# A gated-MLP kernel whose order a planner writes: transposes of the identity in TensorE's planned waits, another clock model in the planner, other due times

## Chip, cores and metric

The kernel runs on one core of one Trainium2 chip. The metric is the device time of one execution in microseconds (us), lower is better; the time before is the median of three runs.

## What is computed

The inputs are float32. Attention over q, k, v of shape (4, 8, 576, 64): heads 0 to 3 see the last 32 positions, heads 4 to 7 every fourth of the last 128. Its output, as 2304 rows of 512, goes through two gated MLPs with inner width 1536:

```python
attn = softmax(where(mask, q @ k.T / 8, -1e9)); x = attn @ v          # rows: (batch, position)
x = x / sqrt(mean(x * x) + 1e-6) * rms_g
x = (silu(x @ w_gate) * (x @ w_val)) @ w_out                          # first MLP
out = (sigmoid(x @ w2_gate) * (x @ w2_val)) @ w2_out                  # second MLP
```

The weights come as 64-bit numbers and are converted to float32 on the chip.

## The kernel before

**The planner.** Nothing is issued in the order in which it is written. Each piece of work is added with `add(engine, cost, fn, reads, writes, tiles, due)` to a `Line`. `emit()` then walks a planned time: for each engine it takes the piece that can start first by the planned costs, among equals the one with the lowest `due`, calls its function, and so fixes the order of that engine's instructions. On the chip the engines run these orders with semaphores; a piece whose data are late holds up all that stands behind it on its engine. A tile comes from a ring of a few buffers and can be taken when its last reader is done. `clocked` lengthens a planned piece of TensorE while the planner believes the engine's clock to be low. All due times and costs that can be set are in `PARAMS`; due times count in planned microseconds from the first MLP step, so that negative ones lie before it.

**The stages.** (1) Attention in 48 groups (batch, pair of heads, third of the sequence). A group is twelve small products for the scores (`scores`, L780), mask and maximum on VectorE (L791), exp on ScalarE (L797), a reciprocal (L804, L805), a scaling (L810), three transposes on TensorE (`turn`, L824) with a copy out (L828), twelve products with v (`values`, L836), and a copy to `xT` (L847, L855). The keys and queries of the first batch are turned by TensorE (`first_qk`, L618 the loads, L631 the transposes, L642 the copies out), those of the other batches by VectorE (`attn_load`, L739, L753). v is loaded at L692 (the dilated heads) and L702, L710 (the others). (2) `x_norm` normalises 384 rows: squares (L880), sums (L896), a reciprocal root on VectorE or GpSimd, spread and turned (L952), then scaled and split in two parts (L964, L488, L492). (3) The first MLP in 6 chunks of 384 rows times 12 steps (`mlp_step`: gate and value products, L1055; `y_group`: output products, L1092). It starts when ten groups are done, and the other groups are woven between its products. (4) The second MLP with a fast product scheme (`unit`, L1240, L1256), then the output.

**Weights.** `words` loads a weight of 512 KB into one of three buffers `wst` (L446, L450), and ScalarE (L466), VectorE (L472 to L481) and then ScalarE and GpSimd (L488, L492) convert and split it. The first twelve have the due times `wload + wload_step * n` for their loads.

**Queues.** Nearly all loads are issued by SyncE (SP), in one order. Those of the first batch have the due times `ld_b` (head pair 3), `ld_a` (head pair 2), `ld_v` (v of the dilated heads), `ld_c` (head pair 0, v 10 later) and `ld_d` (head pair 1, v 6 later).

**Warm-up.** `warm_up` puts 18 products of zeros ahead of all, and offers 19 more lots of five at set times, each of which is dropped if TensorE is busy then.

Of the kernel before, what the change touches and what calls it, by code (L numbers as in the profile page):

```python
# [24 lines left out]
PARAMS = {  # L25
    "margin": 1091.18, "wait": 0.691, "w_sq": 0.926, "w_hi": 1.192, "w_lo": 1.258, "x_hi": 0.315,
    "x_lo": 0.378, "h_hi": 0.2, "h_lo": 0.034, "qk": 0.603, "norm": 0.665, "pts": 12.624,
    "o": 0.023, "snap": 41.721, "h_ahead": 45.667, "h2_ahead": 61.961, "evac": 97.928,
    "holds": (6, 6), "norm_act": 0.209, "slack": 0.0, "share_v": 0.6, "share_p": 0.33, "cold": 1.7,
# [5 lines left out]
    "ld_a": -469.296, "ld_b": -609.198, "ld_v": -251.427, "ld_c": -222.082, "ld_d": -395.339,  # L35
    "lead": -8.213, "xdue": 0.69, "wdue": -6.094, "wslope": 2.935, "wload": -554.115,
    "wload_step": 36.279, "warm_n": 18, "warm_t": 13.382, "warm_dt": 0.858, "warm_c": 19,
    "warm_m": 5, "warm_late": 0.481, "warm_due": 42.437, "mask_cost": 0.18, "exp_cost": 0.36,
    "s_cost": 0.65, "o_cost": 0.56, "t_cost": 0.33,
# [29 lines left out]
class Op:  # L69
    __slots__ = ("eng", "cost", "fn", "tiles", "due", "lat", "preds", "succs", "left", "end",  # L70
                 "seq", "release", "ways", "until", "bus", "ahead", "start", "dense")


class Line:
# [8 lines left out]
    TAIL = {"PE": 0.16, "DVE": 0.085, "ACT": 0.085, "PL": 0.035}  # L83
    AFTER = {"PE": -0.16, "DVE": 0.034, "ACT": 0.034, "PL": 0.078}

    def __init__(self):
        self.ops, self.writer, self.readers = [], {}, {}
        self.now = self.bus = 0.0
        self.last, self.mate, self.longer = {}, {}, 0.0
        self.work, self.window, self.warm = 0.0, 0, True  # L90
# [21 lines left out]
    def clocked(self, start, cost, dense):  # L112

        span = 3.413
# [149 lines left out]
def attention_then_two_gated_mlps(  # L264
# [15 lines left out]
    nc = tc.nc  # L280
# [1217 lines left out]
```

## Time and profile before

| what | value |
| --- | --- |
| runs | 1043.42, 1040.94, 1042.42 us |
| median | 1042.42 us |
| the profiled execution | 1040.54 us, of which its span 1038.8 us |
| TensorE busy | 996.5 us, 96% of the span |
| mean granted clock of TensorE | 0.977 |

The span is the time from the first to the last instruction on the chip; 1.7 us lie around it. A granted clock of 1.00 is TensorE's 2.4 GHz, 0.50 its 1.2 GHz. An engine that counts as busy at the lower clock needs about twice the time for the same work.

### The profile page before, as it was taken

To read this page: it belongs to the slowest core of one execution; us is meant where nothing else is said; L and a number is where in the kernel's file an instruction comes from. 1 tells how busy PE (TensorE), PEld (TensorE's weight loads), DVE (VectorE), ACT (ScalarE), POOL (GpSimd) and SP (SyncE) were. 2 spreads that over 40 slices of the span, in tenths; PEclk is the share of its full clock that TensorE was granted. 3 is DMA by queue.
4 is the path that set the end of the run, shared out by engine and by line. 5 is a ranking of instruction groups with operands and counts; after the bars stand their busy time and mean duration, and the time that the engine had idled before them with its cause. 6 is when DMAs were issued, how large, how long until landed. Compare 5 with 4: busy or idle time off the path is not lost.

```text
span 1038.8 us, 19924 instructions
## 1 busy us (share of the span) xinstructions
PE 996.5 (96%) x7222; PEld 961.8 (93%) x7222; DVE 680.4 (66%) x1461; ACT 468.9 (45%) x1273; POOL 492.6 (47%) x631
## 2 busy tenths in 40 slices
PE   4889989999999999999999989999999999999997
PEld 4768788888999999999999989999999999999996
DVE  5588865476884487767776487558656587466633
ACT  4786755565432443222222455446443354434331
POOL 4365764443732662112213685548545388334410
PEclk9669999999999999999999999999999999999999
DMA  8848646484577476686672332213241334134234
GB/s 184 179 100 202 141 111 161 80 251 111 196 230 263 150 270 220 227 287 230 202 253 84 100 107 75 74 64 112 65 146 60 134 113 155 54 108 122 59 80 92
DMA packets 192978, 152.04 MB, mean 146 GB/s; under 512 B 135760, under 2 KB 164432, under 8 KB 192880
## 3 DMA queue, kind: packets, MB, share of 16 engines
q1 hardware_dynamic: 192880, 150.77, 49.9%
q8 instruction: 57, 0.93, 0.4%
q14 instruction: 41, 0.34, 0.1%
HBM read 103.55 MB, written 47.19 MB: 145 GB/s over the span
## 4 chain that ended last, share of the span: by engine, by line
PE 79%; DVE 6%; SPq 4%; DMA 3%; POOL 3%; issue 2%; ACT 2%; DVEq 0%; POOLq 0%; ACTq 0%
PE y L1092 24%; PE g L1055 13%; PE v L1055 13%; PE att L1240 9%; PE g L1240 7%; PE v L1240 6%; PE att L780 2%; SPq L692 1%; PE att L836 1%; PE att L824 1%; DMA wst<-in_moe_w_val_dram 1%; SPq L618 1%; DVE S L567 1%; DVE t L1272 1%; SPq L739 1%
## 5 line engine op out<-in xcount | busy, mean ns | idle before, releaser
L1092 PE MATMUL y<-h,wo 128*128 128x288 f32 (+1 forms) x2016 | 369.6, 313 | 1.4 <-DVE h L495 1.2
L1092 PEld LDWEIGHTS y<-h,wo 128*128 128x128 f32 x2016 | 318.3, 188 | 3.7 <-DVE h L495 1.5
L492 POOL TENSOR_TENSOR h<-t,h 128x288 fp32r<-128x288 f32 (+1 forms) x131 | 129.1, 987 | 305.0 <-ACT h L488 293.7
L1055 PE MATMUL g<-xo,w 128*128 128x384 f32 x864 | 166.1, 340 | 0.0
L1055 PE MATMUL v<-xo,w 128*128 128x384 f32 x864 | 163.0, 336 | 0.0
L1055 PEld LDWEIGHTS g<-xo,w 128*128 128x128 f32 x864 | 151.7, 190 | 1.9 <-issue 0.4
L1055 PEld LDWEIGHTS v<-xo,w 128*128 128x128 f32 x864 | 150.2, 188 | 0.6
L488 ACT CAST h<-t 128x288 fp32r<-128x288 f32 (+1 forms) x152 | 70.6, 468 | 152.3 <-DVE t L1073 85.3
L1240 PE MATMUL att<-xo,w 128*128 128x288 f32 x576 | 92.1, 295 | 0.0
L1067 ACT ACTIVATE t<-g 128x384 f32<-128x384 f32 x72 | 35.3, 490 | 114.6 <-PE g L1055 114.6
L1240 PEld LDWEIGHTS att<-xo,w 128*128 128x128 f32 x576 | 81.5, 188 | 0.0
L1256 DVE TENSOR_TENSOR t<-t,att 128x288 f32<-128x288 f32 x96 | 43.0, 448 | 51.5 <-PE att L1240 49.6
L1069 DVE SCALAR_TENSOR_TENSOR t<-t,g 128x384 f32<-128x384 f32 x72 | 39.7, 551 | 53.3 <-ACT t L1067 52.8
L810 POOL TENSOR_SCALAR pr<-pr,rs 128x96 f32<-128x96 f32 x115 | 47.2, 427 | 49.5 <-DVE rs L805 37.5
L1240 PE MATMUL v<-xo,w 128*128 128x288 f32 x396 | 63.6, 296 | 3.0 <-DVE t L1256 2.1
L472 DVE TENSOR_SCALAR wz<-wz 128x512 f32<-128x512 f32 x72 | 39.7, 551 | 40.3 <-ACT wz L466 40.2
L492 POOL TENSOR_TENSOR xo<-xq,xo 128x576 fp32r<-128x576 f32 x33 | 50.7, 1544 | 30.6 <-ACT xo L488 18.6
L1240 PE MATMUL g<-xo,w 128*128 128x288 f32 x396 | 63.4, 295 | 0.5 <-DVE t L1256 0.5
L466 ACT ACTIVATE wz<-wst 128x512 f32<-128x512 f32 x71 | 47.4, 668 | 36.3 <-DMA wst<-in_moe_w_gate_dram 14.2
L797 ACT ACTIVATE pr<-pr,nmx 128x96 f32<-128x96 f32 x144 | 52.4, 366 | 19.0 <-DVE nmx L791 19.0
L478 DVE SCALAR_TENSOR_TENSOR wz<-wst,wz 128x512 int32<-128x512 int32 x72 | 59.2, 824 | 1.3
L1240 PEld LDWEIGHTS v<-xo,w 128*128 128x128 f32 x396 | 55.8, 188 | 3.9 <-DVE t L1256 2.8
(164 smaller groups left out, 1625.2 us busy)
## 6 DMA issues: line engine op xcount, KB each, us to landing
z<-wz SPq DMA_DIRECT2D x54, 256.0 KB, 2.5
wst<-in_moe_w_gate_dram SPq DMA_DIRECT2D x24, 512.0 KB, 4.6
wst<-in_moe_w_val_dram SPq DMA_DIRECT2D x24, 512.0 KB, 4.7
wst<-in_moe_w_out_dram SPq DMA_DIRECT2D x24, 512.0 KB, 4.2
xq<-y SPq DMA_DIRECT2D x20, 576.0 KB, 4.6
x<-xo SPq DMA_DIRECT2D x12, 768.0 KB, 4.3
xo<-x SPq DMA_DIRECT2D x12, 768.0 KB, 5.9
z<-z SPq DMA_DIRECT2D x36, 256.0 KB, 2.7
```

Of the source, the lines that this page charges most:

```text
L466: add("ACT", act(CW), lambda: nc.scalar.activation(out=z.t.bitcast(F32), in_=top().bitcast(F32), func=ACTF.Square), reads=[("wst", key)], ...
L472: add("DVE", Shared(0.33), lambda: nc.vector.tensor_scalar(out=z.t.bitcast(F32), in0=z.t.bitcast(F32), scalar1=LEAST * LEAST, scalar2=MANT ...
L478: add("DVE", Shared(0.595), lambda: nc.vector.scalar_tensor_tensor(out=z.t, in0=top(), scalar=-0x40000000, in1=z.t, op0=ALU.bitwise_and, o ...
L488: add("ACT", act(n), lambda: nc.scalar.copy(out=hi(), in_=src()), reads=reads, writes=[key] + [order] * bool(order), tiles=tiles + [dst], ...
L492: add("PL", pool(n), lambda: nc.gpsimd.tensor_tensor(out=lo(), in0=src(), in1=hi().bitcast(F32), op=ALU.subtract), reads=reads, writes=[ke ...
L797: add("ACT", PARAMS["exp_cost"], lambda u=u: nc.scalar.activation(out=pr.t[:, u], in_=pr.t[:, u], func=ACTF.Exp, bias=nmx.t[:, u:u + 1], s ...
L810: add("PL", Shared(0.305), lambda u=u: nc.gpsimd.tensor_scalar(out=pr.t[:, u], in0=pr.t[:, u], scalar1=rs.t[:, u:u + 1], scalar2=1.0, op0= ...
L1055: nc.tensor.matmul(out=bank.t, lhsT=w[:, l, cols], rhs=x[:, r, j], start=kk == 0 and n == 0, stop=kk == KD - 1 and n == 2)
L1069: add("DVE", dve(T1), lambda: nc.vector.scalar_tensor_tensor(out=t.t, in0=t.t, scalar=1.0, in1=gb.t, op0=ALU.add, op1=ALU.mult), writes=[k ...
L1092: nc.tensor.matmul(out=yb.t, lhsT=w.t[:, l, s], rhs=h.t[:, r], start=n == 0 and j == 0, stop=n == nf - 1 and j == 2)
L1240: nc.tensor.matmul(out=bank.t, lhsT=l.t[:, a, cols], rhs=r.t[:, d, j], start=first and j == 0 and m == 0, stop=j == 1 and m == 2, skip_gro ...
L1256: add("DVE", dve(T), lambda: nc.vector.tensor_tensor(out=t.t, in0=t.t, in1=bank.t, op=ALU.add), reads=[(key, uk)], writes=[ck[name]], tile ...
```

## The change

Three things. First, `filler`: where the planner sees that TensorE will stand still ahead of a piece, it puts transposes of the identity into that piece's own PSUM bank (the piece overwrites them), from the time that the bank and the engine are free until 1.645 us (`fill_gap`) before the planned start of the piece, up to the planned time 330. Pieces that may be filled are the turns of keys and queries, scores, turns and values of the groups, the turn of `x_norm`, and the first product of an MLP step. Second, `clocked` counts columns streamed instead of busy time, starts at the low clock, has a phase, and several TensorE costs are set anew (the turn of keys 0.7 to 0.255, scores 0.65 to 0.546, values 0.56 to 0.41, the group's turn 0.33 to 0.265, a change between small and full tiles 0.1 or 0.15); hand-overs from GpSimd are planned at 0.11 and others at 0.06. Third, nearly all numbers in `PARAMS` are other ones, and with them the order on every engine and queue.

```diff
 PARAMS = {
-    "margin": 1091.18, "wait": 0.691, "w_sq": 0.926, "w_hi": 1.192, "w_lo": 1.258, "x_hi": 0.315,
-    "x_lo": 0.378, "h_hi": 0.2, "h_lo": 0.034, "qk": 0.603, "norm": 0.665, "pts": 12.624,
-    "o": 0.023, "snap": 41.721, "h_ahead": 45.667, "h2_ahead": 61.961, "evac": 97.928,
-    "holds": (6, 6), "norm_act": 0.209, "slack": 0.0, "share_v": 0.6, "share_p": 0.33, "cold": 1.7,
-    "low": 0.27, "high": 0.38, "recip": 0.3, "rel1": 182.843, "span1": 47.976, "rel2": 330.435,
-    "span2": 198.646, "ys": 1.139, "ts": 0.072, "cross": 0.055, "same": 0.04, "dma_lat": 1.7,
-    "dma_rate": 330000.0, "by_pe": 0, "turn0": -263.103, "turn1": -120.739, "turn2": -114.354,
-    "att0": -396.426, "span0": 34.624, "lo1": -2.348, "hi1": 21.57, "lo2": 5.46, "hi2": 47.604,
-    "lo3": 22.533, "hi3": 72.028, "lo4": 59.27, "hi4": 110.3, "lo5": 44.19, "hi5": 134.821,
-    "ld_a": -469.296, "ld_b": -609.198, "ld_v": -251.427, "ld_c": -222.082, "ld_d": -395.339,
-    "lead": -8.213, "xdue": 0.69, "wdue": -6.094, "wslope": 2.935, "wload": -554.115,
-    "wload_step": 36.279, "warm_n": 18, "warm_t": 13.382, "warm_dt": 0.858, "warm_c": 19,
-    "warm_m": 5, "warm_late": 0.481, "warm_due": 42.437, "mask_cost": 0.18, "exp_cost": 0.36,
-    "s_cost": 0.65, "o_cost": 0.56, "t_cost": 0.33,
+    "phase": 1.6, "fill_to": 330.0, "fill_from": -0.901, "fill_gap": 1.645, "margin": 311.63,
+    "wait": 0.638, "w_sq": 15.47, "w_hi": 0.883, "w_lo": 0.893, "x_hi": 0.135, "x_lo": 0.995,
+    "h_hi": 1.008, "h_lo": 1.048, "qk": 0.263, "norm": 1.212, "pts": 5.856, "o": 0.0,
+    "snap": 9.942, "h_ahead": 49.205, "h2_ahead": 35.337, "evac": 199.231, "holds": (6, 6),
+    "norm_act": 0.586, "slack": 0.0, "share_v": 0.6, "share_p": 0.33, "cold": 1.7, "low": 0.32,
+    "high": 0.365, "recip": 0.3, "rel1": 174.666, "span1": 86.711, "rel2": 333.22, "span2": 172.23,
+    "ys": 0.233, "ts": 0.0, "cross": 0.06, "same": 0.04, "dma_lat": 1.7, "dma_rate": 330000.0,
+    "by_pe": 0, "turn0": -197.811, "turn1": -225.738, "turn2": -130.544, "att0": -241.711,
+    "span0": 88.054, "lo1": -1.755, "hi1": 21.974, "lo2": 4.013, "hi2": 47.735, "lo3": 44.738,
+    "hi3": 59.513, "lo4": 49.177, "hi4": 86.666, "lo5": 21.121, "hi5": 85.396, "ld_a": -567.186,
+    "ld_b": -685.367, "ld_v": -363.529, "ld_c": -342.394, "ld_d": -345.048, "lead": -17.521,
+    "xdue": 2.751, "wdue": -7.224, "wslope": 2.903, "wload": -514.029, "wload_step": 16.78,
+    "warm_n": 18, "warm_t": 11.124, "warm_dt": 0.527, "warm_c": 19, "warm_m": 5,
+    "warm_late": 0.707, "warm_due": 24.505, "mask_cost": 0.18, "exp_cost": 0.36, "s_cost": 0.546,
+    "o_cost": 0.41, "t_cost": 0.265,
 }
 STEP = 6.24
...
+    CROSS = {"PL": 0.11}
...
-        self.work, self.window, self.warm = 0.0, 0, True
+        self.work, self.window, self.warm, self.quad = 0.0, 0, False, False
...
-    def clocked(self, start, cost, dense):
-
-        span = 3.413
-        w = int(start // span)
+    def clocked(self, start, cost, cols):
+
+        span, at = 3.4133, start + PARAMS["phase"]
+        self.window_at(int(at // span))
+        took = cost if self.warm else cost * 1.95
+        rest = (self.window + 1) * span - at
+        if took > rest:
+            self.work += cols * rest / took
+            self.window_at(self.window + 1)
+            self.work = cols * (1 - rest / took)
+        else:
+            self.work += cols
+        return took
+
+    def window_at(self, w):
         if w > self.window:
-            used = self.work / span if w == self.window + 1 else 0.0
+            used = self.work / (2400 * 3.4133) if w == self.window + 1 else 0.0
             if used < PARAMS["low"]:
                 self.warm = False
             elif used >= PARAMS["high"]:
                 self.warm = True
             self.window, self.work = w, 0.0
-        self.work += cost * (0.92 if dense else 0.6)
-        return cost if self.warm else cost * (1.95 if dense else PARAMS["cold"])
 
     def add(self, eng, cost, fn, reads=(), writes=(), tiles=(), due=0.0, lat=0.0,
-            release=0.0, until=None, other=(), bus=0.0):
+            release=0.0, until=None, other=(), bus=0.0, cols=0, fill=None, quad=False):
...
+            if o.eng == "PE" and o.fill and start < PARAMS["fill_to"]:
+                begin = free["PE"]
+                for t in o.tiles:
+                    if t.t is None:
+                        begin = max(begin, t.ring.free_at() + PARAMS["cross"])
+                if begin > self.writer["ident"].end and start - begin > PARAMS["fill_from"]:
+                    while True:
+                        self.window_at(int((begin + PARAMS["phase"]) // 3.4133))
+                        step = 0.083 if self.warm else 0.166
+                        if begin + step > start - PARAMS["fill_gap"]:
+                            break
+                        self.clocked(begin, 0.083, 128)
+                        begin += step
+                        o.fills += 1
...
-                cost = self.clocked(start, cost, o.dense)
+                if o.quad != self.quad:
+                    cost, self.quad = cost + (0.15 if o.quad else 0.1), o.quad
+                cost = self.clocked(start, cost, o.cols)
             for t in o.tiles:
                 if t.t is None:
                     t.t = t.make()
                     t.ring.taken.append(t)
+            if o.fills:
+                o.fill(o.fills)
...
-                        at = max(p.end + (PARAMS["cross"] if p.eng != e else
+                        at = max(p.end + (self.CROSS.get(e, 0.06) if p.eng != e else
...
+    def filler(bank, rows=P):
+
+        def fill(n):
+            t = bank.t if len(bank.t.shape) == 2 else bank.t.rearrange("p a b -> p (a b)")
+            for _ in range(n):
+                nc.tensor.transpose(t[0:rows, 0:P], ident[:, 0:rows], ident)
+
+        return fill
...
-                add("PE", 0.7, turn, reads=[("raw", nm, hk), "ident"], writes=[("tb", nm, hk, a)],
-                    tiles=[raw, bank], due=turn_due)
+                add("PE", 0.255, turn, reads=[("raw", nm, hk), "ident"], writes=[("tb", nm, hk, a)],
+                    tiles=[raw, bank], due=turn_due, cols=4 * TP, fill=filler(bank))
...
-        some(n, 0.3 * n, -90, 0.0)
+                until=until, cols=n * T)
+
+        some(n, 0.128 * n, -90, 0.0)
         for t in times:
-            some(PARAMS["warm_m"], 0.165 * PARAMS["warm_m"], PARAMS["warm_due"], t,
+            some(PARAMS["warm_m"], 0.128 * PARAMS["warm_m"], PARAMS["warm_due"], t,
...
-            writes=[("sc", gk)], tiles=[pr, sc, qt, kt], due=due)
+            writes=[("sc", gk)], tiles=[pr, sc, qt, kt], due=due, cols=12 * WIN, quad=True,
+            fill=filler(sc))
...
-            writes=[("pt", gk)], tiles=[pr, pt, pts], due=due + 1.87)
+            writes=[("pt", gk)], tiles=[pr, pt, pts], due=due + 1.87, lat=0.08, cols=3 * P,
+            fill=filler(pt, WIN))
...
-            tiles=[pts, vt, o, xT[b]], due=due + 2.5)
+            tiles=[pts, vt, o, xT[b]], due=due + 2.5, cols=12 * QB, quad=True,
+            fill=filler(o))
...
-        add("PE", 0.32, turn, reads=[("rb", c), "ident"], writes=[("rbp", c), "x order"],
-            tiles=[rb, rbp] + xo, due=due)
+        add("PE", 0.247, turn, reads=[("rb", c), "ident"], writes=[("rbp", c), "x order"],
+            tiles=[rb, rbp] + xo, due=due, lat=0.08, cols=3 * P, fill=filler(rbp))
...
-                    tiles=[bank] + xo + [wt[p, f, which, k] for k in range(2)], due=due)
+                    tiles=[bank] + xo + [wt[p, f, which, k] for k in range(2)], due=due,
+                    cols=3 * T1 * len(ks), fill=filler(bank) if ks[0] == 0 else None)
```

## Rows read from the trace of the kernel before

**Rows 1.** The page: granted clock of TensorE in 40 equal slices, in tenths.
```profile
PEclk9669999999999999999999999999999999999999
```

**Rows 2.** Windows: length, busy time (instructions) by engine, clock, DMA share, GB/s.
```profile
14.65:74.30 59.65, 49.86 (x497) 40.49 (x497) 40.99 (x172) 45.94 (x171) 28.83 (x63) 0.70 0.70 145
...
25.10:31.90 6.80, 3.43 (x51) 2.63 (x51) 3.09 (x7) 5.02 (x16) 3.52 (x8) 1.00 1.06 224
...
38.10:59.20 21.10, 21.09 (x187) 17.62 (x189) 12.70 (x60) 15.84 (x55) 8.38 (x21) 0.50 0.64 134
...
74.26:79.70 5.44, 5.44 (x33) 4.34 (x33) 4.37 (x12) 3.69 (x13) 4.19 (x5) 0.50 0.67 186
...
79.70:127.50 47.80, 43.91 (x402) 38.62 (x399) 42.40 (x130) 34.33 (x120) 32.09 (x45) 1.00 0.81 179
127.50:130.90 3.40, 3.40 (x20) 2.76 (x21) 2.01 (x9) 1.70 (x5) 3.10 (x7) 0.50 0.02 5
...
0.00:330.00 330.00, 300.66 (x2474) 269.48 (x2475) 226.03 (x702) 190.15 (x626) 171.42 (x326) 0.93 0.66 171
330.00:1038.80 708.80, 695.80 (x4750) 692.29 (x4748) 454.39 (x760) 278.76 (x647) 321.20 (x305) 1.00 0.43 135
```

**Rows 3.** Waits of TensorE, 0 to 330 us: total, times, longest.
```profile
PE g L631 <- DMA xo<-in_k_dram: 4.0, 1, 4.0
PE att L780 <- ACT qT L642: 3.6, 2, 2.0
PE att L952 <- DVE rb L937: 2.3, 1, 2.3
...
PE att L824 <- DVE nmx L791: 1.6, 1, 1.6
```

**Rows 4.** Timeline of TensorE, 0 to 140 us: start, length, instructions merged.
```profile
5.94 4.69 PE L661 MATMUL y<-h 128*128 128x288 f32 x18 [5.94 <-POOL h L653]
14.65 0.71 PE L631 MATMUL g<-ident,xo 72*128 72x72 f32 x4 [4.02 <-DMA xo<-in_k_dram]
...
30.44 0.71 PE L780 MATMUL att<-kT,qT 64*64 64x96 f32 x12 [2.03 <-ACT qT L642]
...
39.63 1.52 PE L824 MATMUL y<-ident,pr 128*96 128x128 f32 x6
...
74.26 2.29 PE L1055 MATMUL g<-xo,w 128*128 128x384 f32 x6
...
80.54 2.24 PE L1055 MATMUL v<-xo,w 128*128 128x384 f32 x12
...
88.86 0.49 PE L824 MATMUL att<-ident,pr 128*96 128x128 f32 x3
```

**Rows 5.** Timeline of SyncE's queue, 0 to 80 us.
```profile
3.18 1.96 SPq L446 DMA_DIRECT2D wst<-in_moe_w_gate_dram  x1
...
6.31 0.82 SPq L618 DMA_DIRECT2D xo<-in_k_dram  x1
...
14.40 6.75 SPq L692 DMA_DIRECT2D xT<-in_v_dram  x12
...
22.27 0.85 SPq L618 DMA_DIRECT2D pt<-in_k_dram  x1
```

**Rows 6.** Windows: two stretches of one length, all engines.
```profile
25.10:28.50 3.40, 2.72 (x39) 2.11 (x39) 2.07 (x5) 3.09 (x10) 2.11 (x6) 1.00 0.93 176
...
62.60:66.00 3.40, 2.55 (x39) 2.05 (x36) 2.47 (x17) 3.37 (x15) 3.27 (x8) 1.00 0.59 99
```

**Rows 7.** The same stretches, the transposes of L824 alone (TensorE, weight loads).
```profile
25.10:28.50 3.40, 1.21 (x7) 0.64 (x7) 1.00 0.93 176
...
62.60:66.00 3.40, 0.73 (x5) 0.57 (x6) 1.00 0.59 99
```

**Rows 8.** The first of them, the transposes of L631 alone.
```profile
25.10:28.50 3.40, 0.84 (x8) 0.71 (x8) 1.00 0.93 176
```

**Rows 9.** Line L824: duration of one in ns, least/median/most.
```profile
L824 PE MATMUL att<-ident,pr x114: 270/272/449, 58.1 to 263.5; 128*96 128x128 f32 x114
```

More of the change, by code (lines that the diff above doesn't have):

```diff
@@ L70 @@
     __slots__ = ("eng", "cost", "fn", "tiles", "due", "lat", "preds", "succs", "left", "end",
-                 "seq", "release", "ways", "until", "bus", "ahead", "start", "dense")
+                 "seq", "release", "ways", "until", "bus", "ahead", "start", "cols", "fill", "fills", "quad")
 class Line:
@@ L138, in add @@
         o.until, o.bus = until, bus
-        o.dense = "PE order" in writes or writes == ["warm"]
+        o.cols, o.fill, o.fills, o.quad = cols, fill, 0, quad
         preds = set()
@@ L663, in some @@
             add("PE", cost, run, reads=["warm"], tiles=[z, bank], due=due, release=release,
-                until=until)
-        some(n, 0.3 * n, -90, 0.0)
+                until=until, cols=n * T)
+        some(n, 0.128 * n, -90, 0.0)
         for t in times:
-            some(PARAMS["warm_m"], 0.165 * PARAMS["warm_m"], PARAMS["warm_due"], t,
+            some(PARAMS["warm_m"], 0.128 * PARAMS["warm_m"], PARAMS["warm_due"], t,
                  t + PARAMS["warm_late"])
@@ L901, in x_norm @@
         for n, kk in enumerate(order):
-            add("PE", 0.5, lambda kk=kk, n=n: sums(kk, n == 0, n == len(order) - 1),
+            add("PE", 0.586, lambda kk=kk, n=n: sums(kk, n == 0, n == len(order) - 1),
                 reads=[x for x in keys if x[2] == kk] + ["ones"], writes=[("ssp", c)],
@@ L1095, in y_group @@
         add("PE", cost, products, reads=[("wo", layer, f), ("hs", p, c, f)],
-            writes=[("y", p, c, m), "PE order"], tiles=[yb, w, h], due=due)
+            writes=[("y", p, c, m), "PE order"], tiles=[yb, w, h], due=due, cols=1100)
         if n == nf - 1:
@@ L1206, in turn @@
                 nc.tensor.transpose(bank.t[:, m], src.t[:, m, t * TQ:(t + 1) * TQ], ident)
-        add("PE", 0.45, turn, reads=[("sum", p, c, m) for m in range(KD)] + ["ident"],
+        add("PE", 0.45, turn, cols=4 * TQ, reads=[("sum", p, c, m) for m in range(KD)] + ["ident"],
             writes=[("ob", c, t), "PE order"], tiles=[src, bank], due=due)
@@ L1243, in run @@
                                              skip_group_check=not first)
-                add("PE", 0.795, run, reads=[("w", p, f, which, ORDER[i]), xkey[p, b, RIGHT[i]]],
+                add("PE", 0.795, run, cols=1728, reads=[("w", p, f, which, ORDER[i]), xkey[p, b, RIGHT[i]]],
                     writes=[(key, uk), "PE order"], tiles=[bank, l, r], due=at)
```

## The prediction

> **What bounds the kernel now.** I read the page's slices first: TensorE's clock is short of full only in the first eighth of the span and in its last slice [rows 1]. The windows cut the span in two. From 330 us on, TensorE is busy 695.80 of 708.8 us at full clock; the 13.0 us left there hold the tail after the last product too. From 0 to 330 us it is busy 300.66 us at a mean clock of 0.93 [rows 2]. So a planner of the attention stage can win in the first 330 us and hardly anywhere else.
>
> There I went by stretch [rows 2]. From 38.1 to 59.2 us the engine has no pause (21.09 of 21.10 us) at clock 0.50: work that takes half the time at the other level. From 74.26 us the first MLP products run, until 79.7 us still at 0.50: six of them take 2.29 us, twelve take 2.24 us later [rows 4]. From 79.7 to 127.5 us the clock is full, TensorE busy 43.91 and VectorE 42.40 of 47.80 us, the fullest that VectorE gets. Then comes a short fall of the clock, 127.5 to 130.9 us. The record calls the first 25 us full, but no change had been recorded yet: 18 products of 288 columns in 4.69 us, 0.26 us each [rows 4], against 2.24/12 = 0.19 us for 384 columns, show the low level there too.
>
> The waits tell what stands before these stretches [rows 3]: 4.0 us for the first keys, 3.6 us for `qT`, 2.3 us for `rb`, 1.6 us in an L824. After the pause of 2.03 us that ends at 30.44 us [rows 4] the clock fell (full to 31.9 us, 0.50 at 38.1 us [rows 2]).
>
> **Part 1, the transposes themselves.** What one costs is in the rows. At full clock three take 0.49 us and one 0.272 us [rows 4, 9], so each further one (0.49 - 0.27)/2 = 0.11 us; at the low clock six take 1.52 us, the longest single one 0.449 us [rows 4, 9], so (1.52 - 0.45)/5 = 0.21 us. The planner reckons with 0.083 and 0.166 us, so a block lasts 1.3 times as long as planned; with 1.645 us kept free behind it, it stays within any planned wait under some 7 us. Where a wait turns out shorter than planned, the block is on the path. Only waits over 1.73 us (1.645 + 0.083) get any. In the order of before these would be three: 4.02, 2.3 and 2.03 us, with (4.02 - 1.645)/0.166 = 14, 7 and 4 transposes, some 25. Were every idle microsecond after the warm-up planned as one wait, 330 - 300.66 - 5.94 = 23.4 us, it would be 280. The block of 14 is the largest, 14 x 0.166 = 2.3 us: bounds 0 and +2.4 us; I take +0.5, since the plan errs both ways.
>
> What matters more: the longest stretch at the low clock has no wait to be filled. A filler can only act on the pause before it, and there it may fill 0.38 of 2.03 us. So the transposes alone can't carry the change; the order that the new clock model and due times make has to.
>
> **Do transposes hold the clock?** In 25.1 to 28.5 us the engine was busy 2.72 us, of which 1.21 + 0.84 us were transposes [rows 6 to 8], and the clock stayed full. In 62.6 to 66.0 us it was busy 2.55 us, with 0.73 us of transposes [rows 6, 7], and the clock was at 0.50 behind it. The stretch with fewer other products is the one that held, so here transposes seem to count. Against it, the Trainium skill (TensorE: Matmul & The Clock Gate, part 4, PE-mode transpose) says that the full clock doesn't engage for transposes, which don't count as busy in the same way. By that, the filled waits stay empty for the clock; that case is the first rival.
>
> **Part 2, the order of the first loads.** SP issues three weights at 3.18 to 6.3 us and only then the second pair's keys, at 6.31 us [rows 5]. The first turn waits 4.02 us for keys and begins at 14.65 us [rows 4]; the first pair's are due ahead of the weights (`ld_b` -609), so I take it to wait for the second's. The new `ld_a` (-567) lies before `wload` (-514); before, it was -469 behind -554, -518 and -482. So both pairs are issued ahead of all weights, about 3 us earlier and without their bytes in front. The warm-up ends at 10.63 us: at most 4.0 us are won, at least nothing, if the v loads or conversions that move take it. I take -3.0. The v of the dilated heads, first at 14.40 us, moves ahead too (`ld_v` -251 to -363, now before `ld_d`).
>
> **Part 3, the clock from 38.1 to 59.2 us.** At full clock TensorE needs 10.5 us. But ScalarE has 15.84 us of work there and VectorE 12.70 [rows 2]; shared evenly that is 14.3 us. So the bound is 21.1 - 14.3 = 6.8 us, and nothing if the clock isn't kept. I take -4.0: the model now starts at the low clock and counts columns, so its order should avoid some of the fall, and ScalarE's 15.84 us would hold 5.3.
>
> **Part 4, 74.3 to 79.7 us.** TensorE never pauses; at full clock half is saved, 2.7 us. Bounds 0 and -2.7; I take -2.0.
>
> **Part 5, 124 to 135 us.** The waits of 1.6 and 2.3 us [rows 3] and 3.4 us at half clock make 1.6 + 2.3 + 1.7 = 5.6 us. Bounds 0 and -5.6; I take -2.0, as filling would at best keep the clock.
>
> **Part 6, from 330 us on.** `snap`, `evac`, `h2_ahead`, `ys`, `rel2`, `span2` reorder ScalarE and VectorE, but the products wait there for 13.0 us at most. I take 0, and half of 13.0 each way, so -6 and +6, as bounds. The lots of warm-up are dropped where TensorE is busy; one lot of five lasts 5 x 0.26 = 1.3 us, the bound above; I take 0. Nothing else in the diff adds or removes work.
>
> **Sum.** +0.5 - 3.0 - 4.0 - 2.0 - 2.0 = -10.5 us against the profiled execution's 1040.54 us: 1030.0. The median of the runs is 1.9 us above that execution, so 1032 for the median. The best ends together, -4.0 - 6.8 - 2.7 - 5.6 - 6, give 1017.
>
> **Rivals.**
> 1. The fillers leave the clock alone. What remains is part 2 and little of parts 3 to 5: -3 to -6 us, 1038. For it: no wait in the long stretch to fill; the first transposes, at 14.65 us, ran at the low clock and didn't lift it at once. Against it: rows 6 to 8.
> 2. No change. Attention ends earlier, but work that VectorE did in the slow stretch (40.99 us from 14.65 to 74.3 us [rows 2]) moves into 79.7 to 127.5 us, where it has 47.80 - 42.40 = 5.4 us left. If 14.4 us move, 9 us come back as waits of TensorE, which is all of parts 2 to 4: 1042. For it: VectorE's 89% there. Against it: a weight's conversions are due as before (`wdue` -6.1 to -7.2).
> 3. Slower, by weights ahead of attention's loads. `wload_step` 36.3 to 16.8 makes all twelve early weights due between -514 and -329, so ten or eleven come before `ld_c` and `ld_d` (-342, -345); SP takes one as soon as a buffer `wst` is free. One of 512 KB at 224 GB/s (25.1 to 31.9 us, DMA share 1.06 [rows 2]) holds the loads behind it up by 2.3 us. Each that newly comes ahead of head pair 0 (issued at 22.27 us [rows 5]) costs 2.3 us, and TensorE's pause is one more fall of the clock. From five on, 11.5 us, the -10.5 are lost; with seven, 16.1 - 10.5 = +5.6: 1048. For it: the DMA engines are full until then. Against it: three buffers and the conversions let few go ahead.
>
> **Chances.** Forecast 0.54 (1020 to 1037), rival 1 0.16 (1036 to 1040), rival 2 0.11 (within 0.2%, 1040.3 to 1044.5, about what a measurement of this kernel can tell from no change), rival 3 0.19 (above 1044.5). Faster 0.54 + 0.16 = 0.70, same 0.11, slower 0.19. For 8 in 10 the range runs from 1020, below which only nearly all best ends lead, to 1046, into rival 3; the likeliest case alone has 1020 to 1037.
>
> **What the profile after would show.** Right: SP issues two pairs of keys and queries before the first weight; the first L631 starts near 11 us; blocks of transposes of `ident` alone stand ahead of L631, L780, L824 or L952, some tens to two hundred; the clock is full over most of 38 to 60 us; the first L1055 starts some 8 us before 74.26 us at clock 1.00; from 330 us on the products wait as long as before. Wrong: clock 0.50 again where TensorE is busy, although waits before it are filled (rival 1); more waits of L1055 or L1092 for `w`, `h` or `xo` between 80 and 130 us (rival 2); TensorE waiting for DMAs of k, q or v at 20 to 60 us with weights issued in front (rival 3). The prediction fails altogether if the new order moves the stage after 330 us by more than 6 us, of which the diff shows only numbers.

## The result, and the profile after

| | before | after |
| --- | --- | --- |
| median, on one chip | 1041.68 us (4 runs, 1040.87 to 1043.42) | 1033.08 us (4 runs, 1031.78 to 1034.82) |
| ratio, 95% interval | | 0.9916 [0.9894, 0.9939] |
| span of the profiled execution | 1038.8 us | 1033.0 us |

The forecast was 1032 us. The total agrees, several of the terms behind it don't. The changed kernel's lines stand 29 to 42 lower: L631, the turn of keys, is L669; L780 is L818, L824 is L863, L836 is L876, L952 is L993, L1055 is L1096, L1240 is L1282; a filler is L633.

The granted clock on the page of after, in 40 slices (before: [rows 1]):

```profile
PEclk8788899999999999999999999999999999999999
```

Windows of after; columns as in [rows 2]. First up to the first MLP product and from there to the 577th, then single stretches:

```profile
0.00:53.63 53.63, 44.72 (x484) 37.27 (x484) 32.10 (x151) 37.64 (x137) 26.00 (x80) 0.82 0.82 163
53.63:293.00 239.37, 226.04 (x1859) 203.01 (x1857) 182.23 (x544) 134.66 (x435) 139.65 (x254) 0.96 0.64 165
```
```profile
13.40:20.25 6.85, 6.85 (x61) 5.65 (x59) 4.58 (x26) 5.34 (x23) 1.36 (x5) 0.50 0.85 170
```
```profile
40.70:54.40 13.70, 13.03 (x109) 10.12 (x109) 10.93 (x31) 9.92 (x32) 7.23 (x13) 0.50 0.63 147
57.80:64.60 6.80, 6.52 (x21) 5.87 (x21) 6.76 (x22) 3.98 (x16) 5.32 (x8) 0.50 0.59 172
64.60:91.90 27.30, 24.89 (x251) 20.51 (x249) 22.70 (x80) 19.76 (x71) 17.89 (x33) 1.00 0.85 189
122.65:129.50 6.85, 4.20 (x22) 3.67 (x23) 5.34 (x14) 3.76 (x13) 6.44 (x13) 0.50 0.32 68
```

The same two stretches of before, cut at its first and its 577th MLP product:

```profile
0.00:74.26 74.26, 54.50 (x514) 44.82 (x515) 47.14 (x183) 49.29 (x176) 34.98 (x94) 0.76 0.72 153
74.26:300.34 226.08, 216.50 (x1791) 194.99 (x1789) 161.65 (x494) 131.78 (x432) 125.93 (x223) 0.98 0.63 160
```

The windows show one large gain and its partial return. The first MLP product starts at 53.63 us, 20.6 us earlier than at 74.26 [rows 4]. Not all of that is time won. Ahead of this product TensorE has done the turns and values of 15 groups before and of 12 after (45 transposes and 180 products with v, then 36 and 144), and VectorE 47.14 and 32.10 us of work: some of it is put off. The stretch that follows is 239.37 - 226.08 = 13.3 us longer, so 7.3 us are left at the 577th product; the rest of the first MLP then runs at the same pace in both (its last product lies 7.35 us earlier). In the second MLP 2.3 us go again, and the tail is 0.7 us shorter: -7.35 + 2.3 - 0.7 = -5.75 us, which is the difference of the spans. The medians lie 8.6 us apart, for the profiled execution of after (1034.82 us) is the slowest of its four and that of before (1040.54 us) faster than its four; the traces account for 5.75 us.

Timeline of TensorE after, 0 to 140 us (before: [rows 4]):

```profile
6.08 4.41 PE L699 MATMUL y<-h 128*128 128x288 f32 x18 [6.08 <-POOL h L691]
10.33 0.42 PE L669 MATMUL g<-ident,xo 72*128 72x72 f32 x4
...
13.69 1.23 PE L818 MATMUL att<-kT,qT 64*64 64x96 f32 x12
...
53.63 0.69 PE L1096 MATMUL g<-xo,w 128*128 128x384 f32 x1
...
57.99 2.42 PE L1096 MATMUL g<-xo,w 128*128 128x384 f32 x5 [0.80 <-POOL xo L521]
60.21 4.04 PE L1096 MATMUL v<-xo,w 128*128 128x384 f32 x12
...
111.15 2.67 PE L633 MATMUL v<-ident 128*128 128x128 f32 x23
113.58 2.35 PE L1096 MATMUL v<-xo,w 128*128 128x384 f32 x12
...
125.30 0.87 PE L993 MATMUL att<-ident,rb 128*128 128x128 f32 x3 [4.49 <-DVE rb L978]
126.11 1.23 PE L818 MATMUL att<-kT,qT 64*64 64x96 f32 x12
127.26 3.36 PE L1096 MATMUL g<-xo,w 128*128 128x384 f32 x12
```

The first turn waits for nothing any more. The whole program holds 23 transposes as fillers, one block at 111.15 us, in a wait of the MLP and not of attention. The first MLP steps, and the first of chunk 1 behind the wait for `rb`, run at the low clock.

Timeline of SyncE's queue after (before: [rows 5]), and of ScalarE, after and then before:

```profile
1.24 1.02 SPq L656 DMA_DIRECT2D xo<-in_k_dram  x1
...
3.19 1.88 SPq L656 DMA_DIRECT2D xo<-in_k_dram  x1
...
6.67 1.48 SPq L475 DMA_DIRECT2D wst<-in_moe_w_gate_dram  x1
```
```profile
10.78 0.41 ACT L680 COPY kT<-g 128x288 f32<-128x288 f32 x1 [8.78 <-PE g L669]
```
```profile
9.39 0.69 ACT L466 ACTIVATE wz<-wst 128x512 f32<-128x512 f32 x1 [7.39 <-DMA wst<-in_moe_w_gate_dram]
10.88 0.67 ACT L466 ACTIVATE wz<-wst 128x512 f32<-128x512 f32 x1 [0.80 <-DMA wst<-in_moe_w_val_dram]
...
16.53 0.40 ACT L642 COPY kT<-g 128x288 f32<-128x288 f32 x1
```

Both pairs are issued ahead of the first weight, as forecast. ScalarE's order changed too, which the forecast didn't look at: after, its first work is the copy of keys; before, three conversions (L466) and the casts of a split weight (L488) stand ahead of it.

### The profile page after: what moved, and what is told of

The parts are those of the page before. It is cut to its first block, busy times and chain, and to the rows that moved or that the text cites. A ratio compares the mean times of both kernels' runs of the same rounds, so it can differ in the third digit from the quotient of the medians.

```text
span 1033.0 us, 20023 instructions
## 1 busy us (share of the span) xinstructions
PE 997.9 (97%) x7260; PEld 963.8 (93%) x7260; DVE 670.1 (65%) x1446; ACT 465.8 (45%) x1251; POOL 517.6 (50%) x668
## 4 chain that ended last, share of the span: by engine, by line
PE 79%; DVE 6%; POOL 5%; issue 3%; ACT 2%; DMA 2%; SPq 2%; POOLq 0%; DVEq 0%; ACTq 0%
PE y L1134 26%; PE v L1096 13%; PE g L1096 13%; PE att L1282 9%; PE v L1282 6%; PE g L1282 6%; PE att L818 2%; SPq L730 1%; PE att L876 1%; POOL w L521 1%; PE att L863 1%; POOL xo L521 1%; PE y L699 1%; ACT pr L836 1%; DVE t L1314 1%
## 5 line engine op out<-in xcount | busy, mean ns | idle before, releaser
L521 POOL TENSOR_TENSOR h<-t,h 128x288 fp32r<-128x288 f32 (+1 forms) x165 | 162.3, 986 | 307.8 <-ACT h L517 288.9
L1096 PE MATMUL g<-xo,w 128*128 128x384 f32 x864 | 168.0, 342 | 1.9 <-POOL xo L521 1.2
L1096 PE MATMUL v<-xo,w 128*128 128x384 f32 x864 | 164.4, 338 | 0.0
L1096 PEld LDWEIGHTS g<-xo,w 128*128 128x128 f32 x864 | 153.3, 192 | 4.9 <-POOL xo L521 2.7
L1096 PEld LDWEIGHTS v<-xo,w 128*128 128x128 f32 x864 | 152.0, 190 | 0.5
L517 ACT CAST h<-t 128x288 fp32r<-128x288 f32 (+1 forms) x168 | 78.3, 467 | 163.1 <-DVE t L1115 97.7
L1282 PE MATMUL att<-xo,w 128*128 128x288 f32 x576 | 92.1, 295 | 0.0
L1282 PEld LDWEIGHTS att<-xo,w 128*128 128x128 f32 x576 | 81.5, 188 | 0.0
L849 POOL TENSOR_SCALAR pr<-pr,rs 128x96 f32<-128x96 f32 x129 | 51.2, 413 | 59.3 <-DVE rs L844 37.7
L1282 PE MATMUL v<-xo,w 128*128 128x288 f32 x396 | 63.6, 296 | 1.0 <-DVE t L1298 1.0
L1282 PE MATMUL g<-xo,w 128*128 128x288 f32 x396 | 63.3, 295 | 0.1
L1314 DVE SCALAR_TENSOR_TENSOR t<-t,t 128x288 f32<-128x288 f32 x72 | 59.3, 824 | 1.2
L504 DVE SCALAR_TENSOR_TENSOR wz<-wst,wz 128x512 int32<-128x512 int32 x72 | 58.7, 815 | 1.5
L836 ACT ACTIVATE pr<-pr,nmx 128x96 f32<-128x96 f32 x144 | 52.4, 366 | 14.4 <-DVE nmx L830 14.1
L507 DVE SCALAR_TENSOR_TENSOR wz<-wst,wz 128x512 int32<-128x512 int32 x72 | 57.6, 800 | 1.3
```

What stands on the lines that cost most here:

```text
L504: add("DVE", Shared(0.595), lambda: nc.vector.scalar_tensor_tensor(out=z.t, in0=top(), scalar=3, in1=z.t, op0=ALU.logical_shift_left, op1= ...
L507: add("DVE", Shared(0.595), lambda: nc.vector.scalar_tensor_tensor(out=z.t, in0=top(), scalar=-0x40000000, in1=z.t, op0=ALU.bitwise_and, o ...
L517: add("ACT", act(n), lambda: nc.scalar.copy(out=hi(), in_=src()), reads=reads, writes=[key] + [order] * bool(order), tiles=tiles + [dst], ...
L521: add("PL", pool(n), lambda: nc.gpsimd.tensor_tensor(out=lo(), in0=src(), in1=hi().bitcast(F32), op=ALU.subtract), reads=reads, writes=[ke ...
L836: add("ACT", PARAMS["exp_cost"], lambda u=u: nc.scalar.activation(out=pr.t[:, u], in_=pr.t[:, u], func=ACTF.Exp, bias=nmx.t[:, u:u + 1], s ...
L849: add("PL", Shared(0.305), lambda u=u: nc.gpsimd.tensor_scalar(out=pr.t[:, u], in0=pr.t[:, u], scalar1=rs.t[:, u:u + 1], scalar2=1.0, op0= ...
```

## The experiments

Each ratio is to the kernel before on the same chip. Runs 1 to 4, 5 to 8 and 9 to 12 shared a chip each. In runs 1 to 5, 7 and 8 every engine's order is the base kernel's but for the edit shown, in run 11 TensorE's is; in runs 6, 9 and 10 the planner makes a new order on every engine.

**1. No fillers.** Planned, but not issued:

```diff
-            for _ in range(n):
+            for _ in range(0):
                 nc.tensor.transpose(t[0:rows, 0:P], ident[:, 0:rows], ident)
```

> The 23 transposes of the filler, all in one block at 111.15 to 113.58 us, are not issued; the order on every engine and queue is else that of the changed kernel. Theory (the gain comes from the new order, the filler gives nothing): 1033 us, within 1.5 us of the changed kernel, and the next product starts at about 113.6 us as before, since it waits for its weights. Rival A (the block holds the clock): the clock falls behind the pause of 2.4 us and the time rises by 1.7 to 3.5 us, to 1035 or more. Rival B (the block is itself on the path): the time falls by up to 2.4 us, to 1031.

1032.84 us (11 runs), ratio 0.9923 [0.9901, 0.9945]: no difference to after that this can resolve. TensorE's timeline shows that something happens all the same where the block was:

```profile
114.06 0.62 PE L1096 MATMUL v<-xo,w 128*128 128x384 f32 x2 [1.52 <-ACT w L517]
114.88 3.45 PE L1096 MATMUL v<-xo,w 128*128 128x384 f32 x10 [0.20 <-POOL w L521]
```

Without the block the products wait for their weight and then ten take 3.45 us, at the low clock; with it twelve took 2.35 us. So the block fills a real wait and the clock stays up behind it. The last transposes ahead of it (L863) start at 110.89 us in after and 112.11 here, 1.22 us apart; the sums behind the products (L937) at 115.77 and 118.16, 2.39 apart. The block wins 1.2 us at this place. The totals don't show it.

**2. Second pair late.** After, with the second pair's loads (`ld_a`) held until the third weight's load is issued:

```diff
+            count[0] += 1
+            if count[0] == 3:
+                for fn in held:
+                    fn()
...
+            late = (lambda load=load: held.append(load)) if hk == (0, 2) else load
+            dma(late, rows(2 * S, 4 * D), writes=[("raw", nm, hk)], tiles=[raw], due=due, cost=0.6, eng=eng)
```

> The changed kernel with the loads of the second pair of keys and queries issued behind the first three weights again, as before the change; six places of SyncE's queue change, nothing else. Theory (the first turn stood in the chain that sets the end): the first L669 starts at about 14.5 us instead of 10.33, and the time rises by 3 to 5 us, to 1036 to 1038. Rival (later waits take up the difference): the first MLP product starts no more than 1 us later and the time stays within 1.5 us of 1033.

1038.59 us (12 runs), ratio 0.9976 [0.996, 0.9991]: 5.75 us above run 1 on the same chip, 5.5 above the median of after in the result. The first turn is back behind its wait, and the lag stays:

```profile
14.81 0.71 PE L676 MATMUL g<-ident,xo 72*128 72x72 f32 x4 [4.08 <-DMA xo<-in_k_dram]
```

The first MLP product starts at 57.57, the 577th at 296.98 us, 3.9 and 4.0 us later than in after. In after's order this wait lies on the path.

**3. Transposes ahead of chunk 1.** After, with 36 transposes ahead of the turn that waits 4.49 us for `rb`:

```diff
         def turn():
+            if c == 1:
+                for _ in range(36):
+                    nc.tensor.transpose(rbp.t[:, 0], ident, ident)
```

> The changed kernel with 36 transposes of the identity (36 x 0.11 = 3.9 us) put ahead of the turn of the second chunk's normalisation, into the wait of 4.49 us at 120.8 to 125.3 us behind which the clock was low until 129.5 us; else the same order. If transposes hold the clock: full clock over 122 to 130 us, the products from 125.3 to 129.5 us take half, about 2 us less: 1031. If they don't (the first rival of the prediction): the clock falls as it did and the time stays at 1033.

1034.22 us (7 runs), ratio 0.9935 [0.9912, 0.9958].

```profile
118.50 0.57 PE L876 MATMUL att<-pts,v 96*64 96x64 f32 x12
121.00 4.15 PE L994 MATMUL att<-ident 128*128 128x128 f32 x36 [1.93 <-ACT xT L888]
124.99 0.49 PE L996 MATMUL att<-ident,rb 128*128 128x128 f32 x3
125.41 0.71 PE L818 MATMUL att<-kT,qT 64*64 64x96 f32 x12
126.05 2.35 PE L1099 MATMUL g<-xo,w 128*128 128x384 f32 x12
```

The clock holds: twelve scores in 0.71 us and twelve products in 2.35, where after has 1.23 and 3.36. But the block started 1.93 us late, waiting for a copy to `xT`, and ended on the path: from the last values (L876) to the turn it is 124.99 - 118.50 = 6.49 us, in after 125.30 - 120.25 = 5.05 us. VectorE made `rb` from 122.84 us on (L978, 0.55 us), so the turn could have run some 1.5 us earlier. From the last values to the end of the twelve products it is 9.90 us here and 10.37 in after: most of what the clock gave the block took, and the total isn't the 1031 us expected.

**4. Products of zeros in the same place**, 21 of 384 columns (the zeros are set once, on GpSimd):

```diff
+                for _ in range(21):
+                    nc.tensor.matmul(out=rbp.t.rearrange("p t o -> p (t o)"), lhsT=wide[:, 0:P].bitcast(F32R), rhs=wide.bitcast(F32R), start=True, stop=True)
```

> The same place filled with 21 products of zeros, 384 columns each (21 x 0.19 = 3.9 us). Products hold the clock by both theories: full clock over 122 to 130 us and about 2 us less, 1031. Beside the run with transposes this tells whether transposes do as well as products. If neither gains although the clock stays full, the stretch is not bound by TensorE's clock but by what the other engines hand over.

1034.96 us (6 runs), ratio 0.9939 [0.9918, 0.9959]. The block takes 5.48 us from 120.63 us, and the twelve products behind it 2.35 us at 127.01 us. At full clock 21 would take 3.9 us; the records have the low level from 121.1 to 124.6 us, inside this block, where run 3's block of transposes stayed at the full one. Behind both blocks the clock is full. So here transposes did no worse than products; one trace of each can't tell more. As both blocks end on the path, whether the stretch is bound by the other engines stays open.

**5. Queue alone.** Before, with only the three weights' loads moved behind the second pair:

```diff
+        def in_turn():
+            count[0] += 1
+            held.append(load) if count[0] <= 3 else load()
+
+        dma(in_turn, 524e3, writes=["w order", ("wst", key)], tiles=[st], due=load_due,
...
+                count[1] += 1
+                if count[1] == 4:
+                    for fn in held:
+                        fn()
```

> The kernel of before with only the three first weights' loads moved behind the second pair's keys and queries on SyncE's queue; all else in the order of before. Theory A (the place on the queue alone is worth what its undoing cost, 4 to 5.5 us): 4 to 5 us faster than before, ratio 0.995 to 0.996, first L631 at about 10.6 us. Theory B (the queue's order pays only with ScalarE's order): ScalarE's order of before has two weights' conversions ahead of the first copy of the keys, and these now come about 3 us later, so the copies and the scores behind them start no earlier: within 1.5 us of before, or up to 3 us slower.

1042.52 us (11 runs), ratio 1.0014 [1.0002, 1.0027]: nothing won. TensorE's timeline, then ScalarE's:

```profile
10.41 0.68 PE L641 MATMUL g<-ident,xo 72*128 72x72 f32 x4
...
19.77 0.50 PE L641 MATMUL g<-ident,xo 72*128 72x72 f32 x2 [8.21 <-ACT kT L652]
```
```profile
12.20 0.66 ACT L472 ACTIVATE wz<-wst 128x512 f32<-128x512 f32 x1 [10.20 <-DMA wst<-in_moe_w_gate_dram]
...
19.29 0.43 ACT L652 COPY kT<-g 128x288 f32<-128x288 f32 x1
```

The keys are there at 10.41 us, and the next turns wait 8.21 us for the copies: on ScalarE the conversions stand in front, and their weights now land 2.8 us later. The first MLP product starts at 75.91 us.

**6. New planner, old numbers.** After's planner, fillers and costs, with before's numbers for everything that before has in `PARAMS`, except `low`, `high`, `cross`, `s_cost`, `o_cost`, `t_cost`.

> The changed planner (clock by columns, costs, fillers) with the due times and margins of before. Theory (the due times carry the gain, and with the old ones the second pair's loads stand behind the weights again): 1038 to 1046 us, no gain or little. Rival (the clock model carries it): 1035 or less, with the clock full over most of 40 to 60 us.

1048.09 us (7 runs), ratio 1.0071 [1.0044, 1.0097], slower than both ranges. The first MLP product starts at 60.19 us, 14.1 us earlier than before; the first copy of keys at 11.24 us is ahead of the second conversion. The queue is not what did it: SyncE still issues three weights ahead of the second pair, and yet TensorE's first turn waits for nothing:

```profile
6.16 0.82 SPq L718 DMA_DIRECT2D xo<-in_k_dram  x1
```
```profile
10.53 0.68 PE L731 MATMUL g<-ident,xo 72*128 72x72 f32 x4
```

In this order TensorE seems to turn the first pair first (an inference: the trace doesn't name the pair). So the wait of 4.0 us can go without the queue's new order, and an early start of the MLP doesn't need that order either.

But at the 577th 1.4 us are left of it (298.90), and between the last gate and value product of the first MLP and TensorE's end lie 441.0 us, against 434.6 before. The waits of TensorE from 330 us on:

```profile
PE v L1344 <- DVE t L1360: 8.5, 7, 1.8
```

Before had 3.1 us of these. So nearly all of the early start is given back in the first MLP, and what makes the total slower comes from the second.

**7. No lots.** After without the three lots of five warm-up products, which it issues at 17.63, 20.58 and 22.84 us and before never did:

```diff
             def run():
+                if n == PARAMS["warm_m"]:
+                    return
```

> The changed kernel without its three warm-up lots of five products (17.6, 20.6 and 22.8 us), which the kernel of before never issued; the order is else the same. Theory (they help to lift the clock at 20 us): the clock rises a few us later, and the time grows by 1 to 3 us, 1034 to 1036. Rival (they cost what they give, 1.6 us at the low clock and 2 x 0.8 at the full one): within 1 us of the changed kernel, or 1 to 2 us faster.

1033.82 us (12 runs, 1031.58 to 1042.61), ratio 0.9938 [0.9916, 0.996]: the rival's time; the lots neither help nor cost measurably.

**8. Warm-up by transposes.** After, with 21 transposes of the identity for the 18 products of the warm-up:

```diff
+                    while first:
+                        z = first.pop()
+                        for _ in range(21):
+                            nc.tensor.transpose(z.t[:, 0:P], ident, ident)
```

> The changed kernel with its 18 first products of zeros replaced by 21 transposes of the identity of the same length (21 x 0.21 = 4.5 us at the low clock). If transposes lift the clock as products do: the turns from 10.5 us on show the same durations (0.23 us each) at least as often as with products, and the time stays within 1.5 us. If they only hold a full clock but don't lift a low one: the turns take 0.33 us each and the clock is low until 20 us and more, and the time grows by 1 to 4 us.

1033.94 us (6 runs), ratio 0.9932 [0.9914, 0.995].

```profile
6.63 4.74 PE L672 MATMUL y<-ident 128*128 128x128 f32 x21 [6.63 <-POOL ident masks.py:199]
11.17 0.69 PE L675 MATMUL g<-ident,xo 72*128 72x72 f32 x4
...
14.72 0.71 PE L827 MATMUL att<-kT,qT 64*64 64x96 f32 x12
```

21 transposes in 4.74 us are at the low level. Up to 14.72 us TensorE has done nothing but transposes, and the first twelve scores take 0.71 us, which is the full level (1.23 us at the low one). The record has the full level from 12.4 us on. Transposes lift the clock.

**9 and 10. Old planner, new due times.** Before's planner and costs; in run 10 with after's numbers for the early loads (`ld_a` to `ld_d`, `ld_v`, `wload`, `wload_step`), in run 9 also for the attention stage (`turn0` to `turn2`, `att0`, `span0`, `lead`, `xdue`):

```diff
-    "ld_a": -469.296, "ld_b": -609.198, "wload": -554.115, "wload_step": 36.279,
+    "ld_a": -567.186, "ld_b": -685.367, "wload": -514.029, "wload_step": 16.78,
```

> The planner, costs and fill-free code of before, with the due times of after for the early loads (ld_a to ld_d, ld_v, wload, wload_step) and for the attention stage (turn0 to turn2, att0, span0, lead, xdue); all other numbers are before's. Theory: the due times carry the gain whatever planner walks them; the first MLP product then starts before 62 us and the time is 1033 to 1037 us. Rival: the numbers fit only the clock model and costs that they were set with; the time is within 3 us of before's or above it, even if the first MLP product comes earlier, because the order behind it takes the time back.

> As the run before it in this batch, but with the load due times alone. Theory: two pairs of keys and queries ahead of the weights on the queue, and the conversions on ScalarE planned behind them, are worth about the 5.5 us that the late second pair cost: the first turn at 10.4 us, the first scores near 14 us, 1035 to 1038 us. Rival: loads alone move only idle time, as when the queue alone was changed; the first MLP product stays past 70 us and the time is within 2 us of before's.

Run 9: 1056.10 us (5 runs), ratio 1.0148 [1.0126, 1.0171]. Run 10: 1042.16 us (12 runs), ratio 1.0005 [0.9991, 1.0019]. Both rivals. SyncE issues both pairs first in both, and ScalarE again stands in front; its timeline in run 10:

```profile
12.48 0.66 ACT L525 ACTIVATE wz<-wst 128x512 f32<-128x512 f32 x1 [10.47 <-DMA wst<-in_moe_w_gate_dram]
13.87 0.67 ACT L525 ACTIVATE wz<-wst 128x512 f32<-128x512 f32 x1 [0.73 <-DMA wst<-in_moe_w_val_dram]
14.43 0.41 ACT L701 COPY kT<-g 128x288 f32<-128x288 f32 x1
```

The first MLP product starts at 73.26 us in run 10 and 70.98 us in run 9; run 9 loses its time between there and the 577th, which starts at 312.14 us, 11.8 later than before's. With runs 5 and 6: neither half of the change alone is faster than before. That the new due times need the planner that puts the copies first, and that planner the new numbers in both MLPs, is how these runs read together; no run gives the old planner ScalarE's new order alone, or the new planner the old numbers of one stage.

**11. Old `snap`.** After with `snap` 41.721 in place of 9.942. TensorE's order stays; the other engines' changes in the second MLP.

> After with snap at its old value 41.721; TensorE's order stays, ScalarE's, VectorE's and GpSimd's change in the second MLP alone. Theory: the new wait of 2.4 us of a v product for its tanh near 618 us, and the fall of the clock behind it, come from the new snap; both go, and the time falls by 2 to 3.5 us against after, to about 1030 us. Rival: the wait comes from a chain that is late for another reason, or the time is taken up by the next wait; 1033 us as after.

1030.86 us (6 runs), ratio 0.9896 [0.9877, 0.9915]. Waits of TensorE from 330 us on, of after and then of this kernel (its L1344 and L1354 are after's L1282 and L1292):

```profile
PE v L1282 <- ACT t L1292: 2.9, 2, 2.4
PE att L1282 <- ACT t L1292: 2.3, 2, 1.6
```
```profile
PE att L1344 <- ACT t L1354: 2.6, 2, 1.6
PE v L1344 <- DVE t L1360: 0.5, 2, 0.3
```

The wait of the v products is gone, and the time from the last gate and value product of the first MLP to TensorE's end is 432.9 us, in run 12 with the same `snap` 433.0. It was 437.0 in after, 435.9 to 437.8 in the six other traces with after's second MLP, all with a v wait of 2.8 to 3.0 us for the tanh, and 434.6 before. So the new `snap` costs some 3 us. The medians differ by 2.2 us, but were not taken side by side, and the intervals of the ratios overlap.

**12. Put together.** Run 11 without the 23 transposes, with 14 ahead of chunk 1's turn (the edit of run 3 with 14 for 36).

> The snap kernel of this batch, without the block of 23 transposes, and with 14 transposes (some 1.5 us at full clock) ahead of the turn of the normalisation of chunk 1, which waited 4.5 us in the profile of after. Theory: the block ends 3 us before the turn can start, so nothing is behind it, and what it streams keeps the clock full through the first products of chunk 1; 1.5 to 2.5 us below the snap kernel, some 1028 us. Rival: the pause that is left still brings the clock down, or the clock's gain is given back at the next wait; equal to the snap kernel within 1 us.

1029.70 us (6 runs), ratio 0.9894 [0.987, 0.9919]: below before, by the median also below after, and not to be told from run 11. The profile is of the execution that took 1035.98 us; the other five took 1027.94 to 1030.80.

```profile
118.49 3.95 PE L1161 MATMUL v<-xo,w 128*128 128x384 f32 x12 [1.53 <-ACT w L579]
...
128.38 1.75 PE L1056 MATMUL att<-ident 128*128 128x128 f32 x14 [1.06 <-ACT xT L950]
130.83 0.55 PE L1058 MATMUL att<-ident,rb 128*128 128x128 f32 x3 [0.69 <-DVE rb L1040]
131.31 0.71 PE L880 MATMUL att<-kT,qT 64*64 64x96 f32 x12
131.95 2.35 PE L1161 MATMUL g<-xo,w 128*128 128x384 f32 x12
```

This block ends 0.69 us before its turn can start, and the clock is full behind it. Without the 23, the v product at 118.49 us falls to the low level, as in run 1. Both blocks together weren't tried.

## Why the prediction came out as it did

**Part 1, the transposes (+0.5, bounds 0 and +2.4).** One more costs (2.67 - 0.27)/22 = 0.109 us, as worked out; 23 came, some 25 were expected, but in another wait. The block wins 1.2 us at its place (run 1), and nothing that the totals show. That the order must carry the change holds: without a filler (run 1) the gain is the same within the noise.

**Do transposes hold the clock?** Rows 6 to 8 were read rightly: runs 3 and 12 show that transposes hold it, run 8 that they lift it. The rule of the Trainium skill (TensorE: Matmul & The Clock Gate, part 4, PE-mode transpose), that the full clock doesn't engage for them, doesn't hold for these float32 transposes. The first rival's mechanism falls with it, though its observation, little to win by fillers, came true for another reason: there was hardly a planned wait to fill.

**Part 2, the first loads (-3.0, bounds 0 and -4.0).** The wait of 4.0 us went and is on the path (run 2), worth 4.0 us in the trace and 5.5 between medians. But the queue was only half of it: runs 5 and 10 have the queue's order and win nothing, with conversions ahead of the copies of keys on ScalarE, and run 6 loses the wait with the queue's old order. The step from "both pairs are issued ahead of all weights" to "at most 4.0 us are won" looked at TensorE's releaser and not at the engine that works behind it.

**Parts 3 to 5, the clock (-8.0 together).** Their sum was of the right size, their places were wrong. *Part 3* was far too small. The low stretch wasn't cured: after has one at 40.7 to 54.4 us. But the way to the first MLP product lost 19.76 - 8.91 = 10.85 us of TensorE's idle time (74.26 - 54.50 and 53.63 - 44.72). At the low level it was busy for 45.1 us before (32.7 by the records, 12.4 ahead of the first record, where the durations are those of the low level) and 23.1 us after (19.1 and 3.9), so by half of the difference some 11 us more. That is 1.2 us above the 20.6; the halving is rough, three lots of warm-up came, and the turns and values of three groups, at most 3 x (0.49 + 0.57) = 3.2 us at full clock, were put behind this product and not saved. The step that failed is the bound of 6.8 us: it shared out ScalarE's and VectorE's work in the slow stretch as if all of it had to be done there. Up to the first MLP product ScalarE did 49.29 us of work before and 37.64 after, VectorE 47.14 and 32.10.

*Parts 4 and 5* had the wrong sign. Of the 13.3 us that come back up to the 577th product, 13.33 - 9.58 = 3.75 are idle time (239.37 - 226.04 and 226.08 - 216.50). The low clock, 17.6 us against 8.9, gives half of 8.7, so 4.35 us. The other 5.2 us are more busy time counted at full clock. After has 1859 - 1791 = 68 instructions more there: the 23 transposes of the block, of 2.4 us, and the 9 transposes and 36 products with v of the three groups put off, which account for the rest. So about 2.8 us of the return is work that hadn't been saved in the first place. Much of the waits and of the low clock lies where parts 4 and 5 hoped to win. The first MLP steps wait for `xo` and fall to 0.50 (57.8 to 64.6 us). In all eight other traces with after's order in this stage (runs 1 to 4, 7, 8, 11 and 12) the clock is low in some part of 53 to 66 us too. And chunk 1's turn waits 4.49 us for `rb`, where it was 2.3 [rows 3]. A third low stretch, 91.9 to 98.8 us with 6.1 us of busy time, lies where no part looked; before is at full clock there [rows 2]. The return itself is no accident of one profile: from the first to the 577th product it is 12.4 to 14.5 us in all nine traces with after's order.

**Part 6, from 330 us on (0, bounds -6 and +6).** +2.3 us in these traces, within the bounds, and run 11 names the number: `snap`.

**Rivals 2 and 3.** The second rival's premise came true: 47.14 - 32.10 = 15.0 us of VectorE's work moved behind the first MLP product, where it had 14.4. Its price didn't: TensorE's idle time there grew by 3.75 us and not by 9. The waits are for GpSimd's `xo`, for `rb` and for ScalarE's part of `xo`, and VectorE's copy that makes `rb` (L978) itself waited 1.48 us for the reciprocal root on GpSimd. VectorE's load as a cause of the later waits was not tested by itself. The third rival's weights ahead of head pair 0 didn't come: its keys are issued at 18.41 us, 3.9 us earlier than before.

So the total was right by luck: the MLP began 20.6 us earlier, where the forecast had some 8, and most of the difference was paid back behind it, in part in the places where the forecast had put its other gains. Why ScalarE's order flips with the planner is shown by its effect alone; which of the new costs does it was not tried.

## What to carry to other kernels

When a load is brought forward, follow its data through the next engine: if other work stands ahead in that engine's order, the load only waits somewhere else. An early start of the next stage isn't yet time won, since work can have been put behind it; compare the lag at several counted instructions (here the 1st, the 577th and the last) and see where it is given back. Numbers that were set together, costs and due times, can each be worse than the old ones when they are exchanged alone.

## What the runs showed that was not expected

The start of the first MLP product differs between profiles of kernels whose order ahead of it is the same but for small blocks: 50.40 us (run 7), 51.25 to 51.82 (runs 3, 4, 8, 11), 53.63 (after), 54.78 (run 1) and 58.72 (run 12, the execution of 1035.98 us). The records show the low level at other places each time (53.4 to 60.3 us in run 7, 46.7 to 60.4 and 63.8 to 70.6 in run 12). So a single profile can't decide about 3 us in the first 110 us; the time of a later stage, such as that from the first MLP's last gate and value product on, repeats within 2 us and can. And that transposes of the identity lift the clock (21 and the turns of keys in run 8) and hold it (23 in after, 36 in run 3, 14 in run 12).
